# Linear attention on quarter arrays of TensorE, ahead of a leaky-ReLU feed-forward layer

## Chip, core and metric

The kernel runs on one core of a Trainium2 chip. The metric is device time in microseconds; the kernel before takes 296.38 us (median of 3 runs, 295.63 to 297.1). Times inside the kernel come from one profiled execution, whose span is 295.5 us.

## The reference

Inputs are q, k and v of shape (8, 8, 576, 64) (batch, heads, sequence, head dimension), a weight `w_in` (512 x 2048) and a weight `w_out` (2048 x 512), all fp32. The output is (4608, 512).

```python
q_s = exp(q - max(q, -1)); q_s = q_s / (sum(q_s, -1) + 1e-9)      # softmax over the head dimension
k_s = exp(k - max(k, 2));  k_s = k_s / (sum(k_s, 2) + 1e-9)       # softmax over the sequence
kv  = einsum('bhsd,bhse->bhde', k_s, v)                           # 64 x 64 per head
a   = einsum('bhsd,bhde->bhse', q_s, kv)
x   = a.transpose(0, 2, 1, 3).reshape(4608, 512)                  # heads side by side
h   = x @ w_in
out = maximum(0.01 * h, h) @ w_out
```

The kernel computes the exps without subtracting the maxima, which the division cancels.

## The kernel before, in words

**Two layers, tile by tile.** The dense layers work on 9 tiles of 512 tokens; a batch has 576 tokens, so batch b fills the end of tile b and the beginning of tile b+1 (batch 0 fills tile 0 and 64 tokens of tile 1). `emit_moe(t)` does one tile: GEMM1 (L351) makes 16 chunks `ph` of 128 hidden features x 512 tokens, each from four 128x128x512 matmuls over `xT` (features x tokens), and ScalarE evicts each with leaky ReLU into `g_sb` (L381). GEMM2 (L360) makes four blocks `pout` of 128 tokens x 512 features, each from 16 matmuls; VectorE copies each to `out_sb` (L370) and two DMAs store it. That is 128 matmuls of 512 columns in a tile. In tile 0 the first four chunks of GEMM1, and the four blocks of GEMM2, run side by side, since the weights are still arriving.

**Attention of one batch.** The sequence is split as 64 partitions x R = 9 rows. Loads bring q, k and v as fp32. ScalarE takes the exps: q with both heads of a pair beside each other in the free dimension (`make_qexp`, L176), k into a block-diagonal layout, where the upper 64 partitions hold one head and the lower 64 the other and the rest is zero (`make_kexp`, L187, two instructions on 64 partitions each; `clear` writes the zeros once). VectorE casts v to bf16 with a column of ones (L197), and divides q by its row sum (`make_qnorm`, L210 to L212). PE then does three things:

- `make_transpose` (L229): 18 matmuls of 128x128 against an identity bring q to features x tokens in PSUM (`pt`); copies put it into `qT` (L238).
- `make_kv` (L254): for each of 4 pairs of heads, 9 matmuls of 128x128x65 accumulate kv of both heads and, by the column of ones, the sums of k (`pkv`). VectorE takes the reciprocal of the sums (L262) and scales kv into the block-diagonal `kd` (L264).
- `make_out` (L289): for each pair of heads, `kd` times `qT` gives the attention output transposed (`po`), in two pieces, one for each dense tile that it belongs to; ScalarE or VectorE copies it into `xT` (L293).

**What sets the order.** The order is written out by hand (`manual_schedule`): each engine executes in the order in which the code emits, and PE never lets a matmul pass another that waits. `first_attn` emits batch 0, with dummy matmuls on zeros (L172) that keep PE busy while the loads arrive; its last 64 tokens are left to `first_attn_rest`. `slots_of(t)` says which pieces of later batches go where in tile t: the key (1, j) means after chunk j of GEMM1, (2, j) after step or block j of GEMM2. Tile 0 carries the rest of batch 0 and all of batch 1; tile 1 carries batch 2; tiles 2 to 6 carry batches 3 to 7, one piece after each chunk of GEMM1. The exps, divisions and casts of batch t+2 are emitted in GEMM2 of tile t. Tiles 7 and 8 carry nothing.

**Buffers.** PSUM is one pool of 8 banks, each 128 partitions x 2 KB; `ph`, `pout`, `pt`, `pkv` and `po` all take one. A buffer comes back when its last reader has finished; the assignment to buffers is fixed when the program is built.

**Loads.** q, k and v of batch 0 go out on SyncE's queue (half of q on ScalarE's). GpSimd's queue, which converts to bf16 on the way, brings the weights in four quarters each, between them the batches 1 and 2; it starts when k of batch 0 has landed (L142). Batches 3 to 7 go out on SyncE's queue during tiles 1 to 5.

Of the kernel before, what the change touches and what calls it, by code (L numbers as in the profile page):

```python
# [14 lines left out]
LEAKY_SLOPE = 0.01  # L15
# [3 lines left out]
def kernel(  # L19
# [34 lines left out]
    NTS = TT // P  # L54

# [8 lines left out]
    ps_pool = ctx.enter_context(tc.tile_pool(name="ps", bufs=8, space=bass.MemoryType.PSUM))  # L64

    BANK = "bank"

    ctx.enter_context(tc.manual_schedule())

    def new_ld(st, nm):
        st[nm] = ld_pool.tile([P, NG, R * D], FP32, name=f"{nm}_ld", tag="ld")

    def load_q(eng, st, b, gh, h0, h1):
        src = q[b, gh * NG + h0 : gh * NG + h1].rearrange("h (p r) d -> p h (r d)", r=R)
        eng.dma_start(out=st["q"][gh:P:2, h0:h1, :], in_=src)  # L77

    def load_kv(eng, st, b, nm, g0, g1):
        flat = (k if nm == "k" else v)[b].rearrange("h s d -> (h s d)")  # L80
        src = flat.rearrange("(g p f) -> p g f", g=NG, p=P)[:, g0:g1, :]
        eng.dma_start(out=st[nm][:, g0:g1, :], in_=src)

    states = {b: {} for b in range(B)}
    for nm in "qkv":
        new_ld(states[0], nm)
    for h0 in (0, 2):
        load_q(nc.sync, states[0], 0, 0, h0, h0 + 2)
        load_q(nc.scalar, states[0], 0, 1, h0, h0 + 2)
    for nm in "kv":  # L90
        for g0 in (0, 2):
            load_kv(nc.sync, states[0], 0, nm, g0, g0 + 2)
# [9 lines left out]
    for i in range(2):  # L102
        qe = const_pool.tile([P, 2, R, P], BF16, name=f"qe{i}")
        ke = const_pool.tile([P, NG, R, P], BF16, name=f"ke{i}")
        vb = const_pool.tile([P, NG, R, VW], BF16, name=f"vb{i}")
        kd = const_pool.tile([P, NG, P], BF16, name=f"kd{i}")
        qe_buf.append(qe)
        ke_buf.append(ke)
        v_buf.append(vb)
        kd_buf.append(kd)  # L110

    def clear(i):
        nc.vector.memset(ke_buf[i][0:HP, :, :, HP:P], 0.0)
        nc.vector.memset(ke_buf[i][HP:P, :, :, 0:HP], 0.0)
        nc.vector.memset(v_buf[i][:, :, :, D:VW], 1.0)
        nc.vector.memset(kd_buf[i], 0.0)

    clear(0)
# [10 lines left out]
    def emit_w_in(i):  # L129
        nc.gpsimd.dma_start(  # L130
            out=w_in_sb[:, :, i * FQ : (i + 1) * FQ], in_=w_in_r[:, :, i * FQ : (i + 1) * FQ]
        )
# [10 lines left out]
    for i in range(WQ):  # L143
        emit_w_in(i)
    for nm in "qkv":
        new_ld(states[1], nm)
    load_q(nc.gpsimd, states[1], 1, 0, 0, NG)
    load_q(nc.gpsimd, states[1], 1, 1, 0, NG)
    emit_w_out(0)
    emit_w_out(1)  # L150
    load_kv(nc.gpsimd, states[1], 1, "k", 0, NG)
    emit_w_out(2)
    load_kv(nc.gpsimd, states[1], 1, "v", 0, NG)
    emit_w_out(3)

    def load_batch(eng, b):
        for nm in "qkv":
            new_ld(states[b], nm)
        for gh in range(2):
            load_q(eng, states[b], b, gh, 0, NG)  # L160
        for nm in "kv":
            load_kv(eng, states[b], b, nm, 0, NG)
# [5 lines left out]
    def dummies(n):  # L168
        if "t" not in scratch:
            scratch["t"] = ps_pool.tile([P, TT], FP32, name="scr", tag=BANK)  # L170
        for _ in range(n):
            nc.tensor.matmul(scratch["t"], lhsT=wsrc[:, 0:P], rhs=wsrc, start=True, stop=True)  # L172

    def make_qexp(st, b, gl):
        def piece():
            nc.scalar.activation(  # L176
                out=qe_buf[b % 2][:, gl, :, :].rearrange("p r (h d) -> p h r d", d=D),
                in_=st["q"][:, 2 * gl : 2 * gl + 2, :].rearrange("p h (r d) -> p h r d", d=D),
                func=AF.Exp,
            )  # L180

        return piece

    def make_kexp(st, b, g0, g1):
        def piece():
            for lo in (0, HP):
                nc.scalar.activation(  # L187
                    out=ke_buf[b % 2][lo : lo + HP, g0:g1, :, lo : lo + HP],
                    in_=st["k"][lo : lo + HP, g0:g1, :].rearrange("p g (r d) -> p g r d", d=D),
                    func=AF.Exp,  # L190
                )

        return piece
# [10 lines left out]
    def make_qnorm(st, b, gl, r0=0, r1=R):  # L204
        def piece():
            n = 2 * (r1 - r0)
            x = qe_buf[b % 2][:, gl, r0:r1, :].rearrange("p r (h d) -> p (r h) d", d=D)
            qsum = small_pool.tile([P, 2 * R], FP32, name="qsum")
            qrec = small_pool.tile([P, 2 * R], FP32, name="qrec")
            nc.vector.reduce_sum(out=qsum[:, 0:n], in_=x, axis=AX.X)  # L210
            nc.vector.reciprocal(out=qrec[:, 0:n], in_=qsum[:, 0:n])
            nc.vector.tensor_tensor(  # L212
                out=x,
                in0=x,
                in1=qrec[:, 0:n].unsqueeze(2).to_broadcast([P, n, D]),
                op=ALU.mult,
            )

        return piece

    def make_transpose(st, b, gls, r0, r1, copy=None):
        def piece():
            if "qT" not in st:
                st["qT"] = qT_pool.tile([P, NG, S], BF16, name="qT")
            n = r1 - r0
            pt = ps_pool.tile([P, len(gls), n, P], BF16, name="pt", tag=BANK)
            for i, gl in enumerate(gls):
                for r in range(r0, r1):
                    nc.tensor.matmul(  # L229
                        pt[:, i, r - r0, :],  # L230
                        lhsT=qe_buf[b % 2][:, gl, r, :],
                        rhs=ident,
                        is_transpose=True,
                        start=(i == 0 and r == r0),
                        stop=(i == len(gls) - 1 and r == r1 - 1),
                    )
            for i, gl in enumerate(gls):
                (copy or nc.vector.tensor_copy)(  # L238
                    out=st["qT"][:, gl::2, r0 * HP : r1 * HP].rearrange(
                        "c gh (r p) -> c r gh p", p=HP  # L240
                    ),
                    in_=pt[:, i, :, :].rearrange("c r (p gh) -> c r gh p", p=HP),
                )
# [3 lines left out]
    def make_kv(st, b, g0, g1):  # L247
        def piece():
            ke, vb, kd = ke_buf[b % 2], v_buf[b % 2], kd_buf[b % 2]
            n = g1 - g0  # L250
            pkv = ps_pool.tile([P, n, VW], FP32, name="pkv", tag=BANK)
            for g in range(g0, g1):
                for r in range(R):
                    nc.tensor.matmul(  # L254
                        pkv[:, g - g0, 0 : D + 1],
                        lhsT=ke[:, g, r, :],
                        rhs=vb[:, g, r, 0 : D + 1],
                        start=(r == 0),
                        stop=(r == R - 1),
                    )  # L260
            krec = small_pool.tile([P, n, 1], FP32, name="krec")
            nc.vector.reciprocal(out=krec, in_=pkv[:, :, D : D + 1])  # L262
            for lo in (0, HP):
                nc.vector.tensor_tensor(  # L264
                    out=kd[lo : lo + HP, g0:g1, lo : lo + HP],
                    in0=pkv[lo : lo + HP, :, 0:D],
                    in1=krec[lo : lo + HP].to_broadcast([HP, n, D]),
                    op=ALU.mult,
                )
# [11 lines left out]
    def make_out(st, b, g, hi=S, lo=0, copy=None):  # L281
        def piece():
            t, o = divmod(b * S, TT)
            n1 = TT - o
            for c0, c1, tt, oo in ((0, n1, t, o), (n1, S, t + 1, 0)):
                if c0 >= hi or c1 <= lo:
                    continue
                po = ps_pool.tile([P, c1 - c0], FP32, name="po", tag=BANK)
                nc.tensor.matmul(  # L289
                    po, lhsT=kd_buf[b % 2][:, g, :], rhs=st["qT"][:, g, c0:c1], start=True, stop=True  # L290
                )
                cp = copy or (nc.scalar.copy if c0 == 0 else nc.vector.tensor_copy)
                cp(out=xT_of(tt)[:, g, oo : oo + c1 - c0], in_=po)  # L293

        return piece

    def prep_pieces(b, st):
        return [
            make_qexp(st, b, 0),
            make_qnorm(st, b, 0),  # L300
            make_qexp(st, b, 1),
            make_qnorm(st, b, 1),
            make_kexp(st, b, 0, 2),
            make_kexp(st, b, 2, NG),
# [3 lines left out]
    def transpose_pieces(b, st):  # L308
        return [make_transpose(st, b, [gl], 0, R - 1) for gl in range(2)] + [
            make_transpose(st, b, [0, 1], R - 1, R)  # L310
        ]

    def kv_pieces(b, st):
        return [make_kv(st, b, 0, 2), make_kv(st, b, 2, NG)]

    def out_pieces(b, st, copy=None):
        return [make_out(st, b, g, copy=copy) for g in range(NG)]

    def first_attn(st):
        b = 0  # L320
        acopy, dcopy = nc.scalar.copy, nc.vector.tensor_copy
        dummies(24)
        make_qexp(st, b, 0)()
        make_qexp(st, b, 1)()
        make_kexp(st, b, 0, 2)()
# [182 lines left out]
```

## Time and profile before

Tile boundaries are the points at which the chain of work that ended last passes from the second GEMM of one tile to the first of the next. "Busy" is the time in which the engine had at least one instruction running.

| stretch | length, us | PE busy | VectorE busy | ScalarE busy |
|---|---|---|---|---|
| start, up to the first dense matmul (0 to 18.36) | 18.36 | 14.31 | 12.29 | 11.07 |
| tile 0 (18.36 to 50.67) | 32.31 | 32.10 | 18.32 | 18.07 |
| tile 1 (50.67 to 81.76) | 31.09 | 30.84 | 23.43 | 23.65 |
| each of tiles 2 to 6 | 30.75 | 30.6 | 17.35 (10.72 in tile 6) | 16.31 (9.55 in tile 6) |
| tiles 7 and 8 | 27.63, 27.66 | 27.5 | 2.77 | 9.55 |
| end, after the last matmul | 4.70 | 0 | 0.69 | 0 |

How to read it: a stretch whose length equals PE's busy time is bound by PE, and other engines' work lies beside it. In the start no engine is busy throughout, so there the order in which things wait for each other counts. Matmuls overlap in the records: one of 512 columns is on record for 382 ns, and the next begins 216 ns after it.

### The profile page before, as it was taken

The page shows a single profiled execution, that of the slowest core. Times are in us where ns is not written, and L with a number is a line of the kernel's source. Part 1 is how long each engine was busy: PE and PEld are TensorE (multiplying, and loading weights), DVE is VectorE, ACT ScalarE, POOL GpSimd, SP SyncE. Part 2 cuts the span into 40 slices and gives each one's busy share as a digit, 9 for nine tenths or more (in the row PEclk, how much of TensorE's full clock was granted, in tenths as well). Part 3 has the DMA queues.
Part 4 walks back from the last instruction along what each step waited for, and adds up shares of the span by engine and source line. Part 5 has one row for each costly group of instructions (what it writes and reads, how often), then busy time and mean ns, then how long its engine had stood idle before and what let it go on. Part 6 is the DMA issues. An engine that isn't in the chain of part 4 may idle for free.

```text
span 295.5 us, 4092 instructions
## 1 busy us (share of the span) xinstructions
PE 285.1 (96%) x1650; PEld 139.4 (47%) x1681; DVE 140.4 (47%) x240; ACT 146.7 (50%) x206; POOL 12.9 (4%) x23
## 2 busy tenths in 40 slices
PE   8879999999999999999999999999999999999993
PEld 3434455455455445544554455444544444444441
DVE  5862495757955195609660866166731200110020
ACT  4827842994845833485257614681460075016400
POOL 0643200000000000000000000000000000000000
PEclk9979999999999999999999999999999999999998
DMA  6999998892268017901591149313101310230033
GB/s 229 309 206 279 300 343 345 184 388 88 53 186 351 0 40 176 398 9 38 127 390 73 35 106 338 143 37 81 28 2 35 71 35 2 50 84 8 2 71 71
DMA packets 21330, 42.20 MB, mean 143 GB/s; under 512 B 1856, under 2 KB 5952, under 8 KB 21312
## 3 DMA queue, kind: packets, MB, share of 16 engines
q1 hardware_dynamic: 15136, 30.09, 33.3%
q0 software_dynamic: 5888, 11.27, 14.7%
q10 hardware_dynamic: 288, 0.59, 0.6%
q8 instruction: 13, 0.21, 0.3%
q14 instruction: 5, 0.04, 0.0%
HBM read 36.70 MB, written 9.44 MB: 156 GB/s over the span
## 4 chain that ended last, share of the span: by engine, by line
PE 92%; ACT 2%; DMA 2%; issue 1%; SPq 1%; DVE 0%
PE ph L351 42%; PE pout L360 42%; PE pkv L254 3%; PE po L289 3%; PE pt L229 2%; DMA k_ld<-in_k_dram 2%; ACT ke_105 L187 2%; ACT qT L238 1%; SPq L77 1%; DVE out_sb L370 0%; DVE kd_107 L264 0%; DVE krec L262 0%
## 5 line engine op out<-in xcount | busy, mean ns | idle before, releaser
L381 ACT ACTIVATE g_sb<-ph 128x512 bf16<-128x512 f32 x144 | 84.5, 598 | 111.3 <-PE ph L351 108.2
L351 PE MATMUL ph<-xT,w_in_sb 128*128 128x512 bf16 x562 | 133.7, 382 | 0.7
L360 PE MATMUL pout<-w_out_sb,g_sb 128*128 128x512 bf16 x560 | 126.0, 379 | 0.9
L360 PEld LDWEIGHTS <-g_sb 128*128 128x128 bf16 x576 | 56.0, 98 | 66.0 <-issue 0.2
L351 PEld LDWEIGHTS <-w_in_sb 128*128 128x128 bf16 x576 | 55.3, 99 | 59.4 <-issue 2.3
L370 DVE COPY out_sb<-pout 128x512 f32<-128x512 f32 x36 | 24.3, 689 | 107.3 <-PE pout L360 102.7
L238 DVE COPY qT<-pt 128x128 bf16<-128x128 bf16 (+1 forms) x30 | 20.2, 721 | 13.7 <-PE pt L229 13.2
L293 DVE CAST xT<-po 128x64 bf16<-128x64 f32 (+7 forms) x54 | 21.2, 426 | 7.3 <-PE po L289 6.9
L187 ACT ACTIVATE ke_105<-k_ld 64x1152 bf16<-64x1152 f32 x16 | 18.6, 1160 | 1.2 <-DMA k_ld<-in_k_dram 0.9
L187 ACT ACTIVATE ke_109<-k_ld 64x1152 bf16<-64x1152 f32 x16 | 18.6, 1160 | 0.3
L210 DVE TENSOR_REDUCE qsum<-qe_108 128x18 f32<-128x1152 bf16 x8 | 10.8, 1348 | 5.9 <-ACT qe_108 L176 5.8
L210 DVE TENSOR_REDUCE qsum<-qe_104 128x18 f32<-128x1152 bf16 (+2 forms) x10 | 11.1, 1109 | 2.1 <-ACT qe_104 L176 2.0
L293 ACT CAST xT<-po 128x448 bf16<-128x448 f32 (+2 forms) x10 | 4.8, 524 | 13.9 <-PE po L289 13.9
L172 PE MATMUL scr<-wsrc 128*128 128x512 bf16 x32 | 10.4, 491 | 1.2 <-DVE wsrc L95 1.2
L212 DVE TENSOR_TENSOR qe_104<-qe_104,qrec 128x1152 bf16<-128x1152 bf16 (+2 forms) x10 | 11.2, 1118 | 0.3
L212 DVE TENSOR_TENSOR qe_108<-qe_108,qrec 128x1152 bf16<-128x1152 bf16 x8 | 10.9, 1357 | 0.3
L176 ACT ACTIVATE qe_104<-q_ld 128x1152 bf16<-128x1152 f32 x8 | 9.1, 1158 | 1.9 <-DMA q_ld<-in_q_dram 1.8
L289 PE MATMUL po<-qT,kd_107 128*128 128x512 bf16 (+7 forms) x32 | 6.8, 300 | 2.4 <-DVE kd_107 L264 1.3
L176 ACT ACTIVATE qe_108<-q_ld 128x1152 bf16<-128x1152 f32 x8 | 9.0, 1156 | 0.1
L262 DVE RECIPROCAL krec<-pkv 128x2 f32<-128x2 f32 x16 | 2.7, 170 | 10.8 <-PE pkv L254 10.8
L172 PEld LDWEIGHTS <-wsrc 128*128 128x128 bf16 x33 | 3.8, 121 | 6.6 <-issue 3.9
L254 PEld LDWEIGHTS <-ke_105 128*128 128x128 bf16 x144 | 5.5, 97 | 3.0 <-issue 1.7
(39 smaller groups left out, 97.4 us busy)
## 6 DMA issues: line engine op xcount, KB each, us to landing
out_dram<-out_sb SPq DMA_DIRECT2D x72, 128.0 KB, 2.3
q_ld<-in_q_dram SPq DMA_DIRECT2D x10, 576.0 KB, 5.3
k_ld<-in_k_dram SPq DMA_DIRECT2D x5, 1152.0 KB, 8.9
v_ld<-in_v_dram SPq DMA_DIRECT2D x5, 1152.0 KB, 11.1
q_ld<-in_q_dram POOLq DMA_DIRECT2D x4, 576.0 KB, 16.0
k_ld<-in_k_dram POOLq DMA_DIRECT2D x2, 1152.0 KB, 19.0
v_ld<-in_v_dram POOLq DMA_DIRECT2D x2, 1152.0 KB, 18.7
w_in_sb<-in_moe_w_in_dram POOLq DMA_DIRECT2D x4, 512.0 KB, 8.6
```

The lines of the kernel that those rows point to most:

```text
L176: nc.scalar.activation(out=qe_buf[b % 2][:, gl, :, :].rearrange("p r (h d) -> p h r d", d=D), in_=st["q"][:, 2 * gl : 2 * gl + 2, :].rearr ...
L187: nc.scalar.activation(out=ke_buf[b % 2][lo : lo + HP, g0:g1, :, lo : lo + HP], in_=st["k"][lo : lo + HP, g0:g1, :].rearrange("p g (r d) - ...
L210: nc.vector.reduce_sum(out=qsum[:, 0:n], in_=x, axis=AX.X)
L212: nc.vector.tensor_tensor(out=x, in0=x, in1=qrec[:, 0:n].unsqueeze(2).to_broadcast([P, n, D]), op=ALU.mult,)
L238: (copy or nc.vector.tensor_copy)(out=st["qT"][:, gl::2, r0 * HP : r1 * HP].rearrange("c gh (r p) -> c r gh p", p=HP), in_=pt[:, i, :, :]. ...
L254: nc.tensor.matmul(pkv[:, g - g0, 0 : D + 1], lhsT=ke[:, g, r, :], rhs=vb[:, g, r, 0 : D + 1], start=(r == 0), stop=(r == R - 1),)
L289: nc.tensor.matmul(po, lhsT=kd_buf[b % 2][:, g, :], rhs=st["qT"][:, g, c0:c1], start=True, stop=True)
L293: cp(out=xT_of(tt)[:, g, oo : oo + c1 - c0], in_=po)
L351: nc.tensor.matmul(ph, lhsT=w_in_sb[:, cb, j * P : (j + 1) * P], rhs=x[:, cb, :], start=(cb == 0), stop=(cb == NB - 1),)
L360: nc.tensor.matmul(pout, lhsT=g_sb[:, j, tsub * P : (tsub + 1) * P], rhs=w_out_sb[:, j, :], start=(j == 0), stop=(j == NF - 1),)
L370: nc.vector.tensor_copy(out=out_sb, in_=pout)
L381: nc.scalar.activation(out=g_sb[:, j, :], in_=ph, func=AF.Prelu, alpha=LEAKY_SLOPE)
```

## The change

The attention on PE is recast for quarters of the array. A 128x128 PE can be used as four tiles of 64x64, each with its own 64 input partitions and its own 64 output partitions. Heads are 64 wide, so every attention matmul fits one quarter, and the block-diagonal layouts with their zeros are no longer needed.

- **One layout for q, k and v.** All three are loaded so that a group g has head 2g on partitions 0 to 63 and head 2g+1 on partitions 64 to 127. The exps of k become one instruction on 128 partitions, like those of q, and `clear` goes away.
- **Four quarters at once.** `quads(gp)` lists four matmuls, one for each quarter: for the even group of a pair, head 0 goes from the upper input half to the upper output half and head 1 from lower to lower; for the odd group, the halves are swapped. Even groups write one bank, odd groups the other. Transposes, kv and outputs all run in this order; the swap of the second step is undone in the third.
- **PSUM as four pairs of banks.** A buffer is now two banks. GEMM1's chunks are made and evicted two at a time, GEMM2's blocks are copied two at a time (the last two of the last tile alone).
- **Fewer, larger bursts.** In tiles 2 to 6 kv and both transposes of a batch go into one place, and the outputs into another; in tile 1 likewise; in tile 0 there are six places.
- **The start.** ScalarE casts v and VectorE copies the second qT; the outputs of the first half go ahead of the second half's kv. The dummy matmuls become 22 and 9 instead of 24, 7 and 2. The first quarter of w_in is split into two transfers, and batch 0 is loaded on SyncE's queue alone.

```diff
-    ps_pool = ctx.enter_context(tc.tile_pool(name="ps", bufs=8, space=bass.MemoryType.PSUM))
+    ps_pool = ctx.enter_context(tc.tile_pool(name="ps", bufs=4, space=bass.MemoryType.PSUM))
+    def pair(name, dt=FP32):
+        return ps_pool.tile([P, 2, 2048 // mybir.dt.size(dt)], dt, name=name, tag=BANKS)
...
-            for lo in (0, HP):
-                nc.scalar.activation(
-                    out=ke_buf[b % 2][lo : lo + HP, g0:g1, :, lo : lo + HP],
-                    in_=st["k"][lo : lo + HP, g0:g1, :].rearrange("p g (r d) -> p g r d", d=D),
+            nc.scalar.activation(
+                out=(qe_buf if nm == "q" else ke_buf)[b % 2][:, 2 * gp : 2 * gp + 2, :],
+                in_=st[nm][:, 2 * gp : 2 * gp + 2, :],
...
+    def quads(gp):
+        for par in range(2):
+            for lo in (0, HP):
+                yield par, 2 * gp + par, lo, (HP - lo if par else lo)
...
-                    nc.tensor.matmul(
-                        pt[:, i, r - r0, :],
-                        lhsT=qe_buf[b % 2][:, gl, r, :],
-                        rhs=ident,
+            for r in range(r0, r1):
+                for par, g, lo, to in quads(gp):
+                    nc.tensor.matmul(
+                        pt[to : to + HP, par, r * D : (r + 1) * D],
+                        lhsT=qe_buf[b % 2][lo : lo + HP, g, r * D : (r + 1) * D],
+                        rhs=ident[lo : lo + HP, lo : lo + HP],
...
-                    nc.tensor.matmul(
-                        pkv[:, g - g0, 0 : D + 1],
-                        lhsT=ke[:, g, r, :],
-                        rhs=vb[:, g, r, 0 : D + 1],
+                    for par, g, lo, to in quads(gp):
+                        nc.tensor.matmul(
+                            pkv[to : to + HP, par, i * VW : i * VW + D + 1],
+                            lhsT=ke[lo : lo + HP, g, r * D : (r + 1) * D],
+                            rhs=vb[lo : lo + HP, g, r, 0 : D + 1],
...
-        for j in range(J0, NF):
-            ph = ps_pool.tile([P, TT], FP32, name="ph", tag=BANK)
-            for cb in range(NB):
-                gemm1_mm(ph, x, j, cb)
-            act(j, ph)
-            run(1, j)
+        for jj in range(JJ0, NF // 2):
+            ph = pair("ph")
+            for j in (2 * jj, 2 * jj + 1):
+                for cb in range(NB):
+                    gemm1_mm(ph, x, j, cb)
+            act(jj, ph)
+            run(1, jj)
...
-            seq = transpose_pieces(t + 1, st) + kv_pieces(t + 1, st)
-            seq += out_pieces(t + 1, st, nc.vector.tensor_copy)
-            for i, piece in enumerate(seq):
-                put((1, 1 + i), [piece])
+            put((1, 1), [make_kv(st, t + 1)] + transpose_pieces(t + 1, st))
+            put((1, 4), out_pieces(t + 1, st))
```

## The prediction, made before the result was known

> **What bounds the kernel now.** I read the busy shares first, then the chain of work that ended last, then the busy time by stretch, and last the durations by tile shape. PE is busy 96% of the span and holds 92% of the chain, VectorE and ScalarE half of it, so the question is what PE does that is not the two dense layers. I cut the span at the points where the chain passes from one 512-token tile to the next. Columns: stretch, its length, each engine's busy time, PE clock share, DMA share.
>
> ```profile
> 0.00:18.36 18.36, 14.31 (x89) 6.57 (x91) 12.29 (x21) 11.07 (x11) 7.86 (x16) 0.98 0.96 256
> 18.36:50.67 32.31, 32.10 (x193) 15.81 (x196) 18.32 (x39) 18.07 (x27) 5.00 (x7) 0.96 1.11 312
> 50.67:81.76 31.09, 30.84 (x188) 15.45 (x190) 23.43 (x35) 23.65 (x32) 0.00 (x0) 1.00 0.57 173
> ...
> 112.51:143.26 30.75, 30.54 (x187) 15.45 (x190) 17.34 (x29) 16.31 (x22) 0.00 (x0) 1.00 0.47 150
> ...
> 235.51:263.14 27.63, 27.47 (x127) 12.53 (x128) 2.77 (x4) 9.55 (x16) 0.00 (x0) 1.00 0.17 39
> ```
>
> Tile 7, which carries no attention, takes 27.63 us: 128 dense matmuls at 216 ns. Tile 3 takes 30.75, as do tiles 2 and 4 to 6, so the attention of a batch costs 3.12 us of PE. Tile 1 pays 3.46 and tile 0 pays about 3.4 (plus a cold clock). Attention is at most 8 x 3.1 = 25 us. The other part that is not dense work is the start, 18.36 us, where the chain reads (start, us, what):
>
> ```profile
> 2.40 6.27 DMA k_ld<-in_k_dram
> 8.69 1.16 ACT ke_105 L187
> 9.88 1.16 ACT ke_105 L187
> 11.07 1.01 ACT qT L238
> 12.10 1.16 ACT ke_105 L187
> 13.29 1.16 ACT ke_105 L187
> 14.48 1.02 ACT qT L238
> 15.54 0.38 PE po L289
> 15.92 0.58 PE pkv L254 x18
> ...
> 17.38 0.98 PE po L289 x2
> 18.36 6.92 PE ph L351 x26
> ```
>
> The start is a ScalarE queue: four exps of k at 1.16 us each and two evictions of the transposed q, then a second kv block. Within a tile, the chain gives the price of each attention matmul, and the groups by line the ReLU eviction:
>
> ```profile
> 83.48 0.45 PE pt L229 x8
> ...
> 87.08 0.57 PE pkv L254 x18
> ...
> 89.94 0.25 PE po L289 x2
> ```
>
> ```profile
> L381 ACT ACTIVATE g_sb<-ph 128x512 bf16<-128x512 f32 x144 | 84.5, 598 | 111.3 <-PE ph L351 108.2
> L351 PE MATMUL ph<-xT,w_in_sb 128*128 128x512 bf16 x562 | 133.7, 382 | 0.7
> ```
>
> So a transpose is spaced 56 ns, a kv matmul (65 columns) 31.7 ns, and a dense matmul is issued every 216 ns while its record lasts 382: a tail of 0.16 us is normally hidden behind the next one.
>
> **What the skill says.** (1) "TensorEngine Tiling (Array Packing)", Key Properties: 64x64 tiles load weights and multiply independently, but changing the tiling mode drains the engine. (2) "TensorE: Matmul & The Clock Gate", Part 3: packs of tiles ran nearly at once, some 4 ns per further tile, measured at 512 columns; it also says that a weight load overlaps running matmuls only where the row group differs. (3) Tiling page, Restrictions: column tiling turns the fast weight load off. The trace of before has 128x128 work only, so it shows none of the three; its weight loads hide entirely behind the previous matmul, which may cease to hold.
>
> **The change, part by part.**
>
> *PE work.* Per batch 18 transposes, 36 kv and 8 output matmuls become 72, 72 and 16, each on one 64x64 quarter. Four of them, one on each quarter, make a wave. Transposes and kv: 36 waves. Unknown is the length of a wave. If four truly run together it is that of one 65-column matmul, 32 ns (from 0.57/18); if two, 63; if none overlaps, 127. The 4 ns of the page would add up to 12 if waves don't overlap; I take 36. Then 36 x 0.036 = 1.30 us against 1.0 + 1.14 = 2.14. The outputs need half the columns: 0.98 becomes 0.49.
>
> *Mode switches.* Each run of 64x64 work now drains PE on the way in and out. Not shown; between 0 and 2 x (0.16 tail + 0.10 weight load, both from the trace) = 0.52. I take the two tails, 0.33 per burst. Tiles 1 to 6 have two bursts, tile 0 has six (its pieces stay scattered).
>
> *PSUM as four pairs.* A pair of banks comes back only after a 1024-column ScalarE eviction. From 598 ns at 512 columns and 0.81 ns per column (ScalarE evictions of 512 and 384 columns take 586 and 482 ns), that is 1.01 us; with the 0.16 tail and about 0.08 of handing over, 1.25 us after the last matmul of the pair. In tiles 2 to 6 the first dense pair after each burst is given the pair that was filled just before the burst (the third hidden pair takes the second's banks, the sixth the fifth's). PE stands in order, so everything behind it waits: a burst cannot cost less than 1.25 us, whatever its work. For kv and transposes, 1.30 + 0.33 = 1.63, it doesn't bind. For the outputs, 0.49 + 0.33 = 0.82, it does: 1.25. Together 2.88 against 3.12, a gain of 0.24, times 5 = **1.2 us**.
>
> *Tile 1.* Its bursts stand where no such wait binds: 1.63 + 0.82 = 2.45 against 3.46: **1.0 us** gained.
>
> *Tile 0.* 40 waves x 0.036 + 0.49 + 6 x 0.33 = 3.9 against 3.4: **0.5 us** lost. Its weights are not yet the limit: the last quarter of w_out is issued at 24.64 and lands 18.9 us later at 43.5; now it is first needed at about 46.5, and would be at 45.
>
> *The start.* The exp of k covers 128 partitions in one instruction, so two of four disappear (2.3 us of ScalarE); the casts of v go to ScalarE (two, 1.1 each by the slope above), VectorE copies the second qT. Walking the new order with durations of before: exps of q end 7.8; exp k0 8.7 to 9.9; qT 9.9 to 10.9; exp k1 to 12.1; cast v0 to 13.25; kv0 on PE to 13.8; krec and kd (0.17 and 0.29 in the trace) to 14.4; outputs; cast v1 ended 14.4, so ScalarE copies xT 14.9 to 15.9; kv1 to 15.3, its kd 15.9, its outputs 16.3. The dense layer starts near 16.3 instead of 18.36. The first quarter of w_in, issued at 10.25 and landed 5.6 us later, is there at 15.9, and its first half, now a transfer of its own, sooner. **2.0 us** gained.
>
> *At no cost:* the memsets of ke and kd (2.6 us twice) lay beside idle VectorE; the half as many kexps in later tiles and the merged evictions lie on engines that are half idle behind PE; the single q layout moves the same bytes in rows of the same 2304 B. Pout pairs are evicted behind 6.9 us of further matmuls, and the last two stores stay single, so the 4.70 us tail stays.
>
> Sum: 2.0 - 0.5 + 1.0 + 1.2 = 3.7, and 296.4 - 3.7 = **292.7 us**.
>
> **The rivals.**
> *Two at a time.* If weight loads to the same row group wait for its matmul, or slow loads fill the wave, it is 63 ns. Tiles 2 to 6: 2.27 + 0.33 + (0.98 + 0.33) = 3.91, +0.8 each, 4.0; tile 1 +0.45; tile 0: 40 x 0.063 + 0.98 + 2.0 = 5.5, +2.1; start gains 1.3. Sum +5.3: 301.6, slower. For it: the page's clause on row groups, and no wave was ever seen in this trace; against: today's loads run behind their matmul in the same rows.
> *No overlap.* 127 ns: tiles 2 to 6 then pay 4.6 + 0.33 + 2.3 = 7.2, +4.1 each, tile 0 +5.6, tile 1 +3.7, the start nothing: about 326. Only if tiles don't work as the pages say.
> *All free.* 32 ns, no switch cost: tiles 2 to 6 hit the 1.25 floor twice, 2.5, gaining 3.1; tile 1 1.25 + 0.49, 1.7; start 2.1; tile 0 would gain 1.6, but the w_out landing at 43.5 holds it to about 1. Sum 7.9: 288.5.
> *The gain at the start is given back.* Tile 0 lies on a DMA share of 1.11; if the loads land later, or switches cost the full 0.52 (18 bursts x 0.19 = 3.4, of which 5 lie under the floor: 2.5), some 295.2 is left: no change.
>
> **How the numbers follow.** Forecast 0.45 (about 290 to 294.8), all free 0.14, given back 0.13, two at a time 0.20, none 0.08. Faster by over 0.5% (below 294.9): forecast, all free and a quarter of "given back", 0.62. Within 0.5%: most of that rival and the edge of the two-at-a-time, 0.12. Slower: 0.26. The range runs from the all-free end, 288.5, to just beyond two at a time, 302; about 0.15 lies outside.
>
> **What would show it.** Right: records of pt and pkv starting 9 ns apart on average, tile 3 at about 30.5 us with waits of the sixth ph on ScalarE, first dense matmul near 16.3. Wrong: 16 ns or more per record, tile 3 over 31.5; gaps over 0.3 us at the two ends of a burst; a dense layer that waits on w_in or w_out.

## The result and the profile after

The changed kernel takes 292.69 us (median of 4 runs, 292.26 to 293.85), the kernel before 296.74 us in the runs beside it (295.63 to 297.54). The ratio is 0.987, with a 95% interval of 0.983 to 0.992: faster, by 4.05 us, which is clear of the noise. The forecast was 292.7 us. The profiled spans are 290.6 and 295.5 us; they lie further apart than the medians, 4.9 us, in the main because the profiled execution of the kernel before, with 297.32 us, was one of its longer ones.

Busy time by stretch of the changed kernel, cut at the same points as before (columns: stretch, length, busy time and instructions of PE, PE weight load, VectorE, ScalarE and GpSimd, the share of the full clock that PE was granted, DMA share, GB/s). The rows are the start, tiles 0 to 3, tile 6 and tile 7:

```profile
0.00:14.88 14.88, 11.60 (x176) 5.13 (x176) 7.36 (x14) 10.15 (x10) 6.22 (x15) 1.00 0.86 267
14.88:48.40 33.52, 31.49 (x309) 14.04 (x306) 13.19 (x23) 13.78 (x14) 5.90 (x8) 1.00 1.14 297
48.40:78.31 29.91, 29.91 (x289) 14.09 (x290) 22.32 (x26) 16.98 (x17) 0.00 (x0) 1.00 0.57 189
78.31:108.85 30.54, 30.04 (x290) 14.30 (x288) 13.45 (x16) 12.98 (x13) 0.00 (x0) 1.00 0.53 166
108.85:139.38 30.53, 30.03 (x290) 14.24 (x288) 13.44 (x16) 12.98 (x13) 0.00 (x0) 1.00 0.46 151
...
200.41:230.63 30.22, 30.05 (x290) 14.02 (x288) 6.00 (x9) 9.10 (x9) 0.00 (x0) 1.00 0.15 36
230.63:258.26 27.63, 27.63 (x130) 12.51 (x128) 2.45 (x2) 8.19 (x8) 0.00 (x0) 1.00 0.17 39
```

Against the rows of before, the start is 3.48 us shorter, tile 0 is 1.21 *longer*, tile 1 is 1.18 shorter, tiles 2 to 6 are 1.43 shorter together, and tiles 7 and 8 and the tail are the same. That adds up to the 4.9 us between the spans. Two things in these rows were not in the working. Tile 0 is longer although its clock share rose from 0.96 to 1.00, and PE is busy for only 31.49 of its 33.52 us. Tiles 2 to 5 show 0.5 us in which PE does nothing; tile 1 shows none.

The chain of work that ended last says what these idle times are (start, us, what). First the stretch up to the last matmuls of tile 0. It now runs through the loads of the weights, where before it ran through ScalarE and PE:

```profile
2.23 7.06 DMA k_ld<-in_k_dram
...
9.53 2.24 POOL w_in_sb L118 x3
11.78 11.03 DMA w_in_sb<-in_moe_w_in_dram
22.81 0.28 issue
23.10 20.80 DMA w_out_sb<-in_moe_w_out_dram
43.90 0.04 issue
43.94 1.89 PE pout L360 x8
```

The last quarter of w_out is issued at 23.10, as soon as a transfer of w_in ahead of it in GpSimd's queue has landed, and is there 20.8 us later, at 43.9. The matmuls that need it follow within 0.04 us: they had been waiting. In the kernel before it is issued at 24.64 and is there 18.9 us later, at 43.6, so it lands at about the same time in both:

```profile
24.64 0.74 POOL L135 DMA_DIRECT2D w_out_sb<-in_moe_w_out_dram  x1 [1.78 <-DMA w_in_sb<-in_moe_w_in_dram]
```

In tile 3 the chain of the changed kernel reads:

```profile
108.85 3.45 PE ph L351 x16
112.31 0.85 PE pkv L235 x68
113.15 0.68 PE pt L212 x72
113.83 5.30 PE ph L351 x24
119.13 0.02 issue
119.15 1.03 ACT g_sb L384
120.19 0.04 issue
120.23 5.34 PE ph L351 x24
125.57 13.81 PE pout L360 x64
```

Here 72 kv matmuls and 72 transposes take 1.53 us together, and the outputs are not in the chain at all. They lie beside the eviction of 1.03 us that the sixth pair waits for: 1.10 us from 119.13 to 120.23, whatever the outputs cost. (The chain counts from the end of the matmul's record; from the time at which the next dense matmul could have begun, it is 0.16 more.)

The groups by line, form by form, of the changed kernel (busy, mean ns of one, idle time before and its releaser):

```profile
L351 PE MATMUL ph<-xT,w_in_sb 128*128 128x512 bf16 x576 | 128.2, 379 | 3.8 <-ACT g_sb L384 2.0 <-DMA w_in_sb<-in_moe_w_in_dram 1.7 <-DVE xT L283 0.2
L360 PE MATMUL pout<-w_out_sb,g_sb 128*128 128x512 bf16 x576 | 126.5, 379 | 0.3 <-DMA w_out_sb<-in_moe_w_out_dram 0.3
L384 ACT ACTIVATE g_sb<-ph 128x1024 bf16<-128x1024 f32 x72 | 73.6, 1024 | 134.9 <-PE ph L351 134.9
L212 PE MATMUL pt<-ident,qe_102 64*64 64x64 bf16 x288 | 3.8, 196 | 0.2 <-DVE qe_102 L188 0.2
L235 PE MATMUL pkv<-vb_109,ke_108 64*64 64x65 bf16 x288 | 3.3, 193 | 0.0
```

One quarter matmul is on record for 193 ns, yet 288 of them fill only 3.3 us: they overlap. And the dense matmuls of GEMM1 wait 3.8 us, of which 2.0 for ScalarE and 1.7 for w_in, where the same group (L351) waited 0.7 in all before.

### The profile page after: what moved, and what is told of

Its sections match the earlier page's. It is cut to its first block, busy times and chain, and to the rows that moved or that the text cites. A ratio compares the mean times of both kernels' runs of the same rounds, so it can differ in the third digit from the quotient of the medians.

```text
span 290.6 us, 5460 instructions
## 1 busy us (share of the span) xinstructions
PE 278.4 (96%) x2463; PEld 128.9 (44%) x2463; DVE 108.5 (37%) x142; ACT 118.6 (41%) x118; POOL 12.1 (4%) x22
## 4 chain that ended last, share of the span: by engine, by line
PE 79%; DMA 15%; ACT 1%; DVE 1%; POOL 1%; SPq 1%; issue 0%
PE ph L351 39%; PE pout L360 37%; DMA w_out_sb<-in_moe_w_out_dram 7%; DMA w_in_sb<-in_moe_w_in_dram 4%; DMA k_ld<-in_k_dram 2%; PE pkv L235 2%; DMA out_dram<-out_sb 2%; PE pt L212 2%; ACT g_sb L384 1%; DVE out_sb L372 1%; POOL w_in_sb L118 1%; PE po L273 1%; SPq L84 0%; DVE xT L283 0%; SPq L377 0%
## 5 line engine op out<-in xcount | busy, mean ns | idle before, releaser
L351 PE MATMUL ph<-xT,w_in_sb 128*128 128x512 bf16 x576 | 128.2, 379 | 3.8 <-ACT g_sb L384 2.0
L384 ACT ACTIVATE g_sb<-ph 128x1024 bf16<-128x1024 f32 x72 | 73.6, 1024 | 134.9 <-PE ph L351 134.9
L351 PEld LDWEIGHTS <-w_in_sb 128*128 128x128 bf16 x576 | 55.3, 98 | 71.1 <-issue 3.2
L372 DVE COPY out_sb<-pout 128x1024 f32<-128x1024 f32 (+1 forms) x19 | 22.1, 1166 | 80.1 <-PE pout L360 75.1
L283 DVE CAST xT<-po 128x128 bf16<-128x128 f32 (+7 forms) x23 | 13.5, 638 | 28.8 <-PE po L273 28.8
L186 DVE TENSOR_REDUCE qsum<-qe_107 128x18 f32<-128x1152 bf16 x8 | 10.8, 1348 | 16.3 <-ACT qe_107 L161 16.3
L220 DVE COPY qT<-pt 128x1152 bf16<-128x1152 bf16 (+2 forms) x17 | 10.9, 683 | 12.1 <-PE pt L212 12.0
L283 ACT CAST xT<-po 128x1024 bf16<-128x1024 f32 (+3 forms) x8 | 6.8, 849 | 12.7 <-PE po L273 12.7
L161 ACT ACTIVATE ke_108<-k_ld 128x1152 bf16<-128x1152 f32 x8 | 8.8, 1153 | 2.3 <-DMA k_ld<-in_k_dram 2.3
L161 ACT ACTIVATE ke_103<-k_ld 128x1152 bf16<-128x1152 f32 x8 | 9.1, 1156 | 1.1 <-DMA k_ld<-in_k_dram 1.1
L244 DVE RECIPROCAL krec<-pkv 128x4 f32<-128x4 f32 (+1 forms) x9 | 1.6, 179 | 17.7 <-PE pkv L235 17.7
L171 DVE CAST vb_109<-v_ld 128x2304 bf16<-128x2304 f32 x4 | 5.4, 1351 | 2.0 <-DMA v_ld<-in_v_dram 2.0
L187 DVE RECIPROCAL qrec<-qsum 128x18 f32<-128x18 f32 (+2 forms) x18 | 4.6, 254 | 0.6
```

The lines of the kernel that those rows point to most:

```text
L161: nc.scalar.activation(out=(qe_buf if nm == "q" else ke_buf)[b % 2][:, 2 * gp : 2 * gp + 2, :], in_=st[nm][:, 2 * gp : 2 * gp + 2, :], fun ...
L186: nc.vector.reduce_sum(out=qsum[:, :, 0:n], in_=x, axis=AX.X)
L220: (copy or nc.vector.tensor_copy)(out=st["qT"][:, 2 * gp : 2 * gp + 2, r0 * D : r1 * D], in_=pt[:, :, r0 * D : r1 * D],)
L283: copies[0](out=dst, in_=pos[0][:, :, i * n : (i + 1) * n])
L351: nc.tensor.matmul(ph[:, j % 2, :], lhsT=w_in_sb[:, cb, j * P : (j + 1) * P], rhs=x[:, cb, :], start=(cb == 0), stop=(cb == NB - 1),)
L372: nc.vector.tensor_copy(out=out_sb[:, k0:k1, :], in_=pout[:, k0:k1, :])
```

## The experiments

A tile starts here at its first dense matmul on record, up to 0.2 us ahead of the chain's boundary. "Changed" is the changed kernel. Times are us, of each kernel's profile:

| kernel | first dense matmul | tile 0 | tile 1 | tile 3 | tile 6 |
|---|---|---|---|---|---|
| before | 18.15 | 32.36 | 31.08 | 30.75 | 30.75 |
| changed | 14.87 | 33.46 | 29.82 | 30.53 | 30.22 |
| changed, second profile | 15.54 | 33.81 | 29.82 | 30.55 | 30.2 |
| quarter after quarter | 16.48 | 34.28 | 31.67 | 32.22 | 31.9 |
| same rows first | 15.6 | 34.86 | 29.82 | 30.55 | 30.2 |
| outputs in two places | 15.47 | 33.75 | 29.82 | 30.22 | 30.21 |
| k exps in halves | 18.57 | 32.45 | 29.82 | 30.54 | 30.2 |
| k exps in halves, kept warm | 17.87 | 31.08 | 30.43 | 30.56 | 30.2 |
| dummies ahead of dense | 18.89 | 31.07 | 29.82 | 30.53 | 30.21 |
| before, kept warm | 17.99 | 31.01 | 31.08 | 30.75 | 30.75 |
| before, q in rows | 18.47 | 32.7 | 31.09 | 30.75 | 30.75 |
| before, w_in split | 17.68 | 32.56 | 31.09 | 30.75 | 30.75 |
| w_in not split | 15.96 | 31.86 | 29.82 | 30.53 | 30.21 |
| w_in not split, outputs apart | 16.49 | 32.57 | 29.83 | 30.21 | 30.2 |

### How much of the gain is that the four quarters alternate?

Each quarter's nine matmuls follow each other, then the next quarter's; the same for the transposes:

```diff
-                for r in range(R):
-                    for par, g, lo, to in quads(gp):
+                for par, g, lo, to in quads(gp):
+                    for r in range(R):
```

> The transposes and kv matmuls of the changed kernel, with all of one quarter issued before the next quarter begins, so that neighbours in PE's order always share a quarter. Theory (four quarters run at once, and this is what makes the attention cheap): a wave of four goes from about 37 ns to four times the spacing of a single matmul, some 4 x 28 to 32 = 112 to 127 ns, or 2.7 to 3.3 us more in each of tiles 1 to 6, the start and tile 0 longer by 2 to 4 together: 313 to 318 us. Rival (the gain comes from the other parts: one exp of k, fewer and larger evictions, the shorter start): no more than 1 us, 293 to 294 us.

Measured: 306.26 us (2 runs), ratio 1.032 (1.026 to 1.037), slower by 9.75 us than the kernel before beside it (296.51). Two lines from this kernel's chain, in tile 2:

```profile
82.60 3.45 PE ph L351 x16
86.05 1.63 PE pkv L235 x69
```

Here 69 kv matmuls take 1.63 us; in the changed kernel 68 take 0.85. The transposes behind them take as long. For the 72 that are issued, some of which are missing from the records, that is 22.6 ns each, 90 for the four of a wave. The start times say why this is less than four times 32: those of one quarter fit a spacing of some 32 ns, and each quarter's first ones start before the last three or so of the quarter before. In the tiles, alternation is worth 1.69 us in each of tiles 2 to 5, and 1.85 in tile 1. The theory held in kind; the price was set too high.

### Do quarters with the same input rows hinder each other?

```diff
-        for par in range(2):
-            for lo in (0, HP):
+        for lo in (0, HP):
+            for par in range(2):
```

> The changed kernel with the order of the four quarters such that two with the same input rows come one after the other (upper, upper, lower, lower) where they alternated. Theory (quarters are independent of each other): within 0.5 us of the changed kernel, 292.7. Rival (a weight load overlaps running matmuls only where the rows differ): pairs wait for each other, waves of about 63 ns, 1 us more in each of tiles 1 to 6 and some in tile 0: 299 to 301 us.

Measured: 293.68 us, ratio 0.987 (0.984 to 0.991), with tiles 1 and 3 at 29.82 and 30.55, as in the changed kernel. So this order costs nothing within the tiles, which takes away the ground that "two at a time" stood on. Tile 0 of this profile is longer (34.86) because the last quarter of w_out landed later, at 46.03.

### Is it the eviction that sets the price of the outputs?

The third output piece goes behind another chunk pair, so that no pair of banks is wanted back straight after it was filled:

```diff
-            put((1, 4), out_pieces(t + 1, st))
+            outs = out_pieces(t + 1, st)
+            put((1, 4), outs[0:2])
+            put((1, 5), outs[2:3])
```

> Tiles 2 to 6 with the third output piece one pair of chunks later, so that the first dense pair after the outputs gets banks that were free long before. Theory (the burst of outputs is held at 1.10 us by the eviction of the pair before it, where its work is 0.61): two bursts of about 0.45 and 0.35 us take its place, tile 3 goes from 30.5 to about 30.25 us, in sum 1.0 to 1.5 us less: 291.4. Rival (a drain at every change of mode is what the bursts cost): the extra burst adds more than the wait gave, 0.2 to 0.4 us more in each of five tiles: 294.

Measured: 291.8 us (291.15 to 292.48), ratio 0.983 (0.980 to 0.986), the lowest median of all kernels run here. Its chain in tile 3:

```profile
114.79 4.91 PE ph L351 x22
119.70 0.48 PE po L273 x12
120.18 1.83 PE ph L351 x8
122.01 0.26 PE po L273 x4
122.27 0.75 PE ph L351 x3
```

ScalarE has left the chain and the outputs are in it, at 0.74 us. Although PE now changes over to quarters a third time, the tile is 0.31 us shorter (30.22). The floor was real; the changed kernel sat on it in tiles 2 to 5.

### How much does the sooner start bring, and through what?

The first try delays the start: batch 0's k exps in two instructions on 64 partitions each, as before.

```diff
+            if b == 0 and nm == "k":
+                for lo in (0, HP):
+                    nc.scalar.activation(
+                        out=ke_buf[0][lo : lo + HP, 2 * gp : 2 * gp + 2, :],
+                        in_=st[nm][lo : lo + HP, 2 * gp : 2 * gp + 2, :],
+                        func=AF.Exp,
+                    )
+                return
```

> The changed kernel with each exp of batch 0's k cut into two instructions on 64 partitions, as in the kernel before: 2.3 us more on ScalarE in the start. Theory (from the first dense matmul on, tile 0 waits for the loads of w_in and w_out, so a later start is given back there): the first dense matmul 1.2 to 2.3 us later, the end of tile 0 within 0.5 us of 48.4, total within 0.6 us of 292.7. Rival (the start is on the path to the end): all of it arrives, 294 to 295 us.

Measured: 296.03 us (20 runs), ratio 0.998 (0.996 to 1.000): the whole gain is gone, which neither the theory nor the rival expected of a delay of about 2.3 us. PE in the start, by time:

```profile
14.95 0.71 PE L243 MATMUL pkv<-vb,ke 64*64 64x65 bf16 x36 [3.35 <-ACT vb L179]
16.26 0.64 PE L281 MATMUL po<-qT,kd 64*64 64x512 bf16 x4 [0.60 <-DVE kd L253]
16.68 0.71 PE L243 MATMUL pkv<-vb,ke 64*64 64x65 bf16 x36
17.99 0.64 PE L281 MATMUL po<-qT,kd 64*64 64x512 bf16 x4 [0.60 <-DVE kd L253]
18.57 0.61 PE L359 MATMUL ph<-xT,w_in_sb 128*128 128x512 bf16 x1
```

The cast of v stands behind the exps on ScalarE, so PE waits 3.35 us for it. After that everything is longer: kv 0.71 against 0.48, and the first dense matmuls are spaced 0.43 us instead of 0.216. Spacings twice as long say that PE ran at half clock. "TensorE: Matmul & The Clock Gate", Part 1, has these two spacings (426.7 and 215.7 ns at 512 columns) and puts the drop after an idle window of some 3.4 us; the wait of 3.35 us is close to that.

So the next kernels separate clock from delay. The kernel of the last experiment gets fourteen dummy matmuls ahead of its first kv block, and the kernel *before* gets four dummies behind the first output and four behind the second kv block:

```diff
         make_out(st, b, 0, TT, 0, dcopy)()
+        dummies(4)
         make_out(st, b, 1, TT, 0, acopy)()
         make_kv(st, b, 2, NG)()
+        dummies(4)
         make_out(st, b, 2, TT, 0, dcopy)()
```

> The kernel with the first exps of k in halves (296.0 us), and fourteen dummy matmuls in the 3.35 us for which PE then stands idle ahead of the first kv. Theory (it lost 3.3 us because PE cooled in that gap, on top of a start that is late): the clock is up at the first dense matmul, kv and outputs of the start run at 0.48 and 0.41 us again, and 1.5 to 2 us come back: 294.2. Rival (the whole loss is the later start): within 0.5 us of 296.0.

> The kernel before with four dummy matmuls in each of two gaps that PE has in the start, so that its clock stays up; nothing else is changed. Theory (a part of what the change gained lies in the clock: the kernel before enters the dense layer at half clock and loses 8 x 0.21 = 1.7 us there, the changed one enters it warm): 1 to 1.7 us less than before, 295.0. Rival (the clock at the start plays no part): same as before, or up to 1 us more for the dummies.

Measured, halves kept warm: 294.87 us, ratio 0.992 (0.989 to 0.996), 1.2 us below the cold one, or 1.8 if each is set against the kernel before beside it (ratios 0.998 and 0.992); kv takes 0.48 again. Measured, before kept warm: 295.8 us, ratio 0.996 (0.994 to 0.998), 1.25 us below the kernel before beside it, and tile 0 takes 31.01 instead of 32.36. In its chain, the first dense matmuls come 0.216 us apart:

```profile
18.16 3.88 PE ph L353 x18
```

So the kernel before loses about 1.2 us by entering tile 0 at half clock, eight dummies take that away, and this much of the distance between the two kernels is not attention at all.

The granted clock of each execution, on average over its span, tells more. Of the kernel before beside this experiment, 19 executions were granted 0.992 or less and have a median of 297.37 us, and 16 were granted 0.995 or more and have 295.65. All 13 of the warmed one are at 0.996 or more: the dummies do not make a warm execution faster, they prevent the cold ones. The changed kernel shows a third of this difference at most, within its scatter: its thirteen executions have a median of 293.4 us at 0.994 or less (6) and 292.7 at 0.997 or more (7), and those of the version with the outputs in two places 291.8 in both groups (2 and 4). Its second profile shows how: tile 0's first seven dense matmuls run at half clock, yet tile 0 still ends with a wait for w_out.

```profile
15.54 5.15 PE L351 MATMUL ph<-xT,w_in_sb 128*128 128x512 bf16 x16
44.96 1.89 PE L360 MATMUL pout<-w_out_sb,g_sb 128*128 128x512 bf16 x8 [0.25 <-DMA w_out_sb<-in_moe_w_out_dram]
```

PE at half clock then only arrives later at a wait that it would have had anyway. The halves kept warm, whose tile 0 waits for no load, show the difference again: three executions at 0.994 or less took 296.0 to 296.1 us, the four others 293.8 to 294.9. Why this profile has the cold matmuls and the first one none, though no wait ahead of them is longer than 1.1 us, stays open.

Then the start alone is delayed in the changed kernel, by eight dummies ahead of the first dense matmul:

```diff
         make_out(st, b, [1], 0, TT, (acopy, dcopy))()
+        dummies(8)
```

> The changed kernel with eight dummy matmuls (8 x 0.216 = 1.7 us) on PE right before the first dense matmul; the clock stays up. Theory (PE then waits 1.65 us for w_in and 0.3 for w_out in tile 0, so a later start is absorbed by these waits): the waits on w_in shrink by 1.7 in sum, the end of tile 0 stays, total within 0.4 us of the changed kernel, 292.7 to 293.1. Rival (the start is on the path to the end): 1.7 us more, 294.4.

Measured: 293.97 us, ratio 0.989 (0.986 to 0.991), between the theory and its rival; but the delay was larger than planned. The dummies ran partly at half clock and k came 0.5 us later than in the changed kernel's first profile, so the dense layer starts at 18.89, 4.0 us later than there, while tile 0 ends only 1.63 later (49.96 against 48.33). Tile 0 takes 31.07 us, with no wait for a load. The matmuls on the last quarter of w_out begin at 45.56, 26.7 us after the first dense one:

```profile
18.90 8.80 PE L352 MATMUL ph<-xT,w_in_sb 128*128 128x512 bf16 x40
...
45.56 1.90 PE L361 MATMUL pout<-w_out_sb,g_sb 128*128 128x512 bf16 x7
```

The halves kept warm, whose tile 0 waits for no load either, give 26.7 too. In the changed kernel's first profile this would be 14.87 + 26.7 = 41.5, and the quarter lands at 43.9. So 2.4 us of its sooner start are slack: tile 0 cannot end before the weights are there. And 31.07 against 31.01 of the warmed kernel before is what PE does in tile 0 with and without the change: no difference.

One part of the start could be tried in the kernel before by itself, loading q in the layout of k and v (each head's q then meets another head's kv, so the attention computed is not the reference's):

```diff
-        src = q[b, gh * NG + h0 : gh * NG + h1].rearrange("h (p r) d -> p h (r d)", r=R)
-        eng.dma_start(out=st["q"][gh:P:2, h0:h1, :], in_=src)
+        flat = q[b].rearrange("h s d -> (h s d)").rearrange("(g p f) -> p g f", g=NG, p=P)
+        g0, g1 = h0 + (h1 - h0) // 2 * gh, h0 + (h1 - h0) // 2 * (gh + 1)
+        eng.dma_start(out=st["q"][:, g0:g1, :], in_=flat[:, g0:g1, :])
```

> The kernel before, with q loaded in the layout of k and v (128 partitions in a row) in as many transfers of the same bytes as before; q's heads then meet other heads' kv, so the output is another. Theory (in the changed kernel k landed 0.8 us sooner because q no longer goes to every other partition): k lands and the first exp of k starts 0.5 to 0.8 us sooner, total 0.5 to 0.8 us less than before. Rival (landing times differ from run to run, the layout does nothing): same as before.

Measured: 295.95 us (22 runs), ratio 0.997 (0.995 to 1.000), 0.8 +- 0.7 us. Sorted by granted clock as above, both groups are a little shorter than the kernel before: 295.08 against 295.65 at 0.995 or more, 296.88 against 297.37 at 0.992 or less. So the layout brings something, some 0.5 us. That k lands sooner by it is not shown: the first exp of k starts at 8.33 here and at 8.69 in the kernel before, but at 8.39 and 8.44 in two other profiles with the old layout. The first exp of q starts at 4.25, in those three at 4.88 to 5.31.

### Why do the weights land too late?

> The changed kernel with the first quarter of w_in loaded by one transfer again. Theory (tile 0 of the changed kernel ends when the last weights land, and these are late because the two halves of the first quarter moved only some 120 KB per us for about 4.5 us, where the kernel before moved 205 from the start): the queue runs at about 205 KB per us at once, the last quarter of w_out lands 1.5 to 2 us sooner, tile 0 ends near 46.8, total 1 to 1.7 us less: 291.3. Rival (the half that comes first is what lets the dense layer begin; the slow stretch has another cause): same or later, 292.7 to 293.5.

> The kernel before with the first quarter of w_in in two transfers, as in the changed kernel. Theory (the split itself slows the first 4 us of the weights): the weights' queue moves 110 to 150 KB per us for about 4 us and 205 after; the last quarter of w_out lands 1 to 2 us later than 43.5, which PE, that needs it at 46.5, hardly notices: total within 0.5 us of before. Rival (the slow stretch comes from the other changes, such as q's layout or ScalarE's queue): 205 KB per us from the beginning.

```diff
-    emit_w_in(0, 0, 2)
-    emit_w_in(0, 2, 4)
+    emit_w_in(0)
```

The first kernel takes the split of w_in's first quarter out of the changed kernel, as shown; the second puts the same split into the kernel before, and nothing else. What all transfers moved from 12 to 17 us, in order: before, changed, before with the split, changed without it.

```profile
DMA packets 921, 0.95 MB, mean 191 GB/s; under 512 B 27, under 2 KB 892, under 8 KB 921
```

```profile
DMA packets 665, 0.67 MB, mean 133 GB/s; under 512 B 30, under 2 KB 664, under 8 KB 664
```

```profile
DMA packets 636, 0.63 MB, mean 125 GB/s; under 512 B 40, under 2 KB 623, under 8 KB 636
```

```profile
DMA packets 931, 0.95 MB, mean 191 GB/s; under 512 B 18, under 2 KB 927, under 8 KB 930
```

With the split, either kernel moves a third less in these 5 us, and it is the split, since alone in the kernel before it does the same. The packets themselves are only a little slower. Those of GpSimd's queue took 114.9% of the 16 engines' time for 881 packets before, and 85.6% for 612 with the split, which is 104 and 112 ns a packet (100 and 116 in the changed kernel without and with it): mostly, the engines were given fewer. What gives them fewer is open. Counted from GpSimd's go-ahead (its copy of `gate`), the last quarter of w_out is issued 14.51 us later in the kernel before (10.13 to 24.64) and 16.99 with the split (9.87 to 26.86); in the changed kernel 13.75 with the split (9.35 to 23.10) and 12.35 without it (9.68 to 22.03). At this point the split costs the queue 1.4 to 2.5 us. Of the landing it takes less. Counted from the first issue of w_in, the last quarter of w_out is there after 33.3 us before and 35.1 with the split, and after 34.4 us in the changed kernel and 33.6 without it: 0.8 to 1.8 us.

The total shows little of it. Changed without the split: 292.64 us, ratio 0.989 (0.983 to 0.994), 0.6 below the changed kernel beside it, inside the noise. The forecast of 291.3 was missed: w_out landed at 43.4, only 0.5 us sooner than in the changed kernel's first profile instead of 1.5 to 2, and tile 0 ended at 47.8 instead of 46.8. The split is thus a part of the lateness and not the whole of it. Its first dense matmul now waits for the whole quarter, at 15.96:

```profile
15.96 3.41 PE L350 MATMUL ph<-xT,w_in_sb 128*128 128x512 bf16 x15 [0.46 <-DMA w_in_sb<-in_moe_w_in_dram]
```

Tile 0 is then 1.6 us shorter than in the changed kernel's first profile (31.86), but starts 1.09 later. So an early half costs later loads, and a late whole costs the start. Before with the split: 297.06 us, a single run, with nothing to be told from the kernel before's 296.48. Its w_out lands at 45.1, and the matmuls that need it begin at 45.8 without a wait for it: the dense layer starts late enough there.

The two edits that helped a part, together (no split, outputs in two places), beside the changed kernel again:

> Both edits that helped or should: w_in not split, and the third output piece of tiles 2 to 6 one pair of chunks later. Theory: the two gains lie in different tiles and add, 1 to 1.7 plus 0.3 x 5 = 1.5 (four tiles at 0.3 in the trace): about 290 us. Rival (sooner loads move other stretches onto waits): no better than the outputs alone, 291.8.

> The changed kernel once more, on the same chip as the others of this set: 292.7, for comparison.

Measured: together 293.01 us (290.09 to 293.59), ratio 0.987 (0.982 to 0.993); changed again 293.26, ratio 0.989 (0.985 to 0.993). Tiles 2 to 6 are at 30.2, as they should be, but the forecast of 290 was missed, since the start gives the gain back:

```profile
16.50 10.30 PE L350 MATMUL ph<-xT,w_in_sb 128*128 128x512 bf16 x40 [1.08 <-DMA w_in_sb<-in_moe_w_in_dram]
```

It waits 1.08 us for w_in and then runs its first seven dense matmuls at half clock, 40 matmuls taking 10.30 us instead of some 8.8. Here tile 0 has no wait for w_out that would hide the half clock, and the six executions fit that: the only one with a granted clock above 0.992 took 290.09 us, the five others 292.3 to 293.59. One execution is no proof. The outputs in two places alone have the lowest ratio, 0.983, against 0.987 and 0.989 of the changed kernel; that this version is faster than the changed kernel as a whole, and not in its tiles only, is not settled, since the intervals overlap.

## Why the prediction was right, step by step

**Tiles 2 to 5: right, and shown.** A gain of 0.24 each was forecast, from 2.88 us of attention; the tiles show 30.53 - 27.63 = 2.90, a gain of 0.22. The eviction floor that the working found from the order of banks is in the chain as 1.10 us, 1.26 with the tail of 0.16 that the forecast of 1.25 includes, and taking its cause away brought 0.31. In tile 6 the floor does not bind, which the working missed: there the first dense pair after the outputs gets the banks of an output piece that VectorE has copied, and the tile gains 0.53.

**The wave: right.** 36 ns were taken; in tiles 2 to 6 the records have 36 for kv and 40 for transposes in the mean, and 33 between undisturbed waves of kv. The four starts of a kv wave lie 3 to 4 ns apart, as the "some 4 ns" of "TensorE: Matmul & The Clock Gate", Part 3, has it for 512 columns; transposes start 3 to 9 ns apart. That page's clause on row groups does not show: the experiment with the same rows first would have shown it. "No overlap" and "two at a time" are refuted; even quarter after quarter gives 90 ns, not 127.

**The change of mode: in kind right, too dear.** 0.33 us per burst were taken. Tile 1 holds two bursts and no wait, and costs 29.82 - 27.63 = 2.19 for work of some 1.79 (0.71, 0.59 and 0.49), so 0.2 per burst. The first matmul on a quarter follows the last dense one by 0.31 us, where in the kernel before the first attention matmul follows by 0.216, as any dense one would; about as much is lost on the way out. With the cheaper change tile 1 gained 1.26 instead of 1.0. Since a burst cost the kernel before nothing at its ends, having fewer of them brings nothing by itself.

**Tile 0's work: wrong in size.** +0.5 us was forecast; warm and without waits it is 31.07 against 31.01, +0.06. The waves are short and the changes cheap.

**The start: right in kind, too small.** The first dense matmul was put at 16.3; it is at 14.87, in other profiles of the same start at 15.5. The walk took the landing times of before; q and k came 0.7 to 0.8 us sooner in this profile (the exp of k at 7.88 instead of 8.69), and ScalarE's four instructions from there to the first cast's end took 4.2 us instead of 4.55.

**"Its weights are not yet the limit": the step that failed.** The last quarter of w_out was reckoned to land at 43.5 and to be needed at 45. The landing was nearly right: 43.9. The need was not: without a wait it would have come at 41.5, because the start is sooner than forecast, PE enters tile 0 at full clock, and the attention in tile 0 is cheaper. The landing takes 43.9 - 41.5 = 2.4 us of this back, which is also 33.46 - 31.07 of tile 0. On record it is spread over three waits, 1.65 us for w_in and 0.26 for w_out, each with a tail of 0.16 ahead of it. The split of w_in had been counted as a help only; it made w_in slow and cost the last landing 0.8 us, but the kernel without it waits for w_out as well (needed at 15.96 + 26.7 = 42.6, landed at 43.4). A dense layer that waits on w_in or w_out had been named as a sign of being wrong, and it showed. It is the rival "given back", which came true in part.

**Not in the working: the clock.** Before's tile 0 has a clock share of 0.96, which the prediction noted and then left out of the sum. It cost that profile 1.35 us, and over the executions of the kernel before some 1.2 (297.05 against 295.8 when kept warm).

Start and tile 0 together were forecast at -1.5 and are -2.2 in the first profile, -1.2 in the second. Three gains were larger than forecast or not in the sum at all, the start (3.28 on record instead of 2.0), the clock (1.35) and tile 0's work (0.44), together 3.1; the landing of w_out took 2.4 of them back. That the two sides nearly cancel was luck: the working had none of this excess and no such wait. The gain of tiles 1 to 6 (2.7 us in the profiles, 2.2 forecast) is what the reasons really carried.

## What to carry to other kernels

Heads of 64 on quarters of PE pay when the four quarters alternate matmul by matmul: grouped by quarter, the same work made the kernel slower than it had been on the full array. With fewer, larger PSUM buffers, ask of each burst which buffer the next matmul gets: if it was filled just before, the eviction sets the price, and work moved in between is free. A sooner start counts only until the last load that is waited for, so work out when each load is needed after the change, not only when it lands. And PE's clock on entering a stretch counts only where no such wait follows.

## What the runs showed of the hardware that was not expected

- Matmuls on one quarter start some 32 ns apart, yet at a change to another quarter the starts of some three of them mix: 22.6 ns a matmul when quarters follow each other, about 8 to 12 when they alternate.
- With a transfer that converts to bf16 cut into two, of two blocks each, all queues together moved 125 to 133 GB/s over the 5 us behind it, where with one transfer of four blocks they moved 191; the packets took 7 to 16% longer, and there were 28 to 31% fewer.
- The last quarter of w_out was issued between 22.0 and 24.6 us in the kernel before, the changed kernel and the one without the split, and landed between 43.4 and 43.9 in all three: what was issued sooner took longer.
- One program entered its dense layer at full clock in one profile and at half clock in another, with waits of at most 1.1 us ahead of it. In the kernel before the half clock cost 1.35 us of tile 0; in the changed kernel, where tile 0 ends with a wait for weights, little or nothing.
